# Deltanet and a SiLU feed-forward on one core: the keys of chunk 0 read in long runs, their lengths on GpSimd, and the diagonal blocks taken from PSUM

## The chip, the core and the metric

The kernel runs on one core of a Trainium2 chip. The metric is the device time of one execution in microseconds (us). The core has a matrix engine (TensorE, PE in the profile, its weight loads PEld), a vector engine (VectorE, DVE), a scalar engine (ScalarE, ACT), a general engine (GpSimd, POOL) and a queue engine (SyncE, SP). Each runs its own instructions in order and waits for the others through semaphores. SBUF holds tiles of up to 128 partitions; PSUM receives what TensorE computes.

## What is computed

Four batches of eight heads, 768 tokens, 48 channels a head. For each head a state of 48x48 is carried along the tokens; keys are divided by their lengths:

```python
k_n = k / (np.linalg.norm(k, axis=-1, keepdims=True) + 1e-06)
for t in range(S):
    y[:, :, t] = q_t @ state
    state = state + beta_t * outer(k_t, v_t - state @ k_t)
x = y as 3072 tokens x 384;  h = x @ w_in;  g = h * sigmoid(h);  out = g @ w_out
```

w_in is 384x2048 and w_out 2048x384, both float32.

## The kernel before, in words

**Tiling.** The tokens are cut into 6 chunks of 128 (C, NCH). Inside a chunk the recurrence is solved as a matrix problem: per head a triangular 128x128 system made of k's scores, the lengths and beta is inverted, and then applied to v, to the state and to the queries. The inverse starts from blocks of 32x32 tokens (T) on the diagonal, four to a chunk (NB), and joins them. Chunks 1 to 5 overlap with the feed-forward, whose matmuls (`phid`, L1088, and the output products at L1200) keep TensorE filled to the end of the kernel. Chunk 0 has nothing to overlap with, and the change is in its first part.

**Who sets the order.** The order of instructions on each engine is written out by hand: `pin` (L78) chains an instruction behind the one before it on its engine, `in_line` and `issue` (L92, L101) chain the DMAs on SP's queue (or put one on ACT's). `busy(n)` (L343, L347) issues n matmuls of 128x384 whose results nobody reads. `pin` also counts TensorE's instructions, and the list `loads` (L1504) starts weight and query fetches from the third weight fetch on at given counts, by `paced`.

**Chunk 0's first part (L1445 to L1538).** k comes by six DMAs on SP (`load_pair`, L144) with a token on each partition and a head's 48 floats (192 bytes) as a run, into `kbufs[0]`, whose rows are padded from 48 to 64. beta comes by six DMAs on ACT's queue. Then, in this order of data: POOL squares k (L385); DVE adds up the squares over the channels (`add_squares`, L389) and does sixteen small instructions for lengths and steps (`norm_steps`, L395 to L426, among them the reciprocal at L419, the product at L423 and the transpose of the step at L426); TensorE transposes k with its padding (`turn`, L510) into PSUM, ACT and DVE copy that out (L524, L522); TensorE forms the scores of k with k in 64x64 blocks (`first_score`, `score`, L539); ACT and DVE copy them from PSUM to SBUF (L554, L557); POOL and ACT copy the 32x32 diagonal blocks out of these copies into `stage` (`diagonal_blocks`, L564); DVE turns them so that each partition holds one block of one head (`turn_diagonal`, L578). beta is turned to tokens by a matmul and an ACT copy (`beta_of`, L361, L364).

**The inverse.** `invert_first` (L692) runs on DVE: a multiply by the step (L697), then 15 rank-1 steps of a multiply (L705) and an add each, on both 16x16 halves of every block at once; two transposes (L720 the second); meanwhile TensorE transposes queries and keys of chunk 1 and the dummies of `busy` fill its gaps after steps 9, 11, 13 and 14. Then come the joins on TensorE, each with copies by ACT and DVE behind it: `corner` (L743, the masked adds at L750), `turned` (L759), `straight` (L772), `merge_half` (L832), and then the inner products (L866) and the first outputs (L910). In between ACT, DVE and POOL split the weights into parts ("narrowing": ACT at L233 and L234, POOL at L246), one piece of the weights after another, as they land.

**SP's queue in the first 50 us:** k of chunk 0 (6 DMAs), q (6), the first weight fetch, k of chunk 1 (6), the second weight fetch, v (8), and, at counts of TensorE, the third and fourth weight fetches and the next q.

## Time and profile before

| what | us |
|---|---|
| median of 3 runs | 633.36 (632.27 to 634.15) |
| the profiled execution | 633.96 |
| its span | 631.8 |

The profiled execution is one more run, with the profiler on. Its span goes from the first to the last record; 2.16 us lie around it. The times on the timeline count from the span's start. The mean granted TensorE clock was 0.989 of full speed.

How to read the lines further down: a line of a timeline has start, duration, engine, line of the kernel, operation, output and inputs by the program's names with partitions x elements, and how many instructions it stands for; in brackets the engine's idle time before it and what ended that. Tiles share memory, so one name can stand for several uses: `stage` and `sums_of_w` hold chunk 0's blocks in the first part. One matmul in float32 shows as two records, a transpose as one. A line of the windows has a stretch, its length, the busy time of PE, PEld, DVE, ACT and POOL (number of records), the granted clock (1.00 is full), the busy share of the DMA engines and GB/s; narrowed to one line, it has PE and PEld alone. A line of the chain of waits has start, duration and what the end of the kernel, followed back, hung on. A DMA line of the page has the count, KB each and the median us from issue to landing.

### The profile page before, as it was taken

How to read it: one execution, taken by the hardware profiler on the slowest of the kernel's cores; microseconds unless marked ns; L12 is line 12 of the kernel's file. 1: busy time of each engine (PE TensorE's matmuls, PEld its weight loads, DVE VectorE, ACT ScalarE, POOL GpSimd, SP SyncE). 2: the span in 40 equal slices, each digit the busy share in tenths (PEclk: the TensorE clock that was granted, in tenths of full speed). 3: DMA queues.
4: the chain of work that ended last, by engine and by line, in shares of the span. 5: the costliest groups of instructions: out<-in, count | busy, mean ns of one | idle time of the engine just before them, and what ended most of it. 6: DMA issues, size and time to landing. Idle time of an engine off the chain costs nothing.

```text
span 631.8 us, 21374 instructions
## 1 busy us (share of the span) xinstructions
PE 617.7 (98%) x9390; PEld 543.3 (86%) x9390; DVE 415.5 (66%) x927; ACT 226.7 (36%) x516; POOL 94.0 (15%) x101
## 2 busy tenths in 40 slices
PE   8889989999999999999999999999999999999997
PEld 5578778666799989989989989989989989988997
DVE  6886779999667974546975554976444983345432
ACT  4657873332441122451122451122452122454210
POOL 5234631335020020020020010020002000000000
PEclk9869999999999999999999999999999999999999
DMA  9656506350459360459141359433254024010011
GB/s 175 134 141 199 170 16 149 116 86 4 101 100 186 62 108 4 95 107 188 34 92 20 72 125 156 65 75 44 52 113 95 2 75 62 17 38 1 0 26 26
DMA packets 136941, 52.61 MB, mean 83 GB/s; under 512 B 108672, under 2 KB 130432, under 8 KB 136848
## 3 DMA queue, kind: packets, MB, share of 16 engines
q1 hardware_dynamic: 136512, 51.09, 39.6%
q8 instruction: 74, 1.21, 0.9%
q10 hardware_dynamic: 336, 0.15, 0.1%
q14 instruction: 19, 0.16, 0.1%
HBM read 39.09 MB, written 9.96 MB: 78 GB/s over the span
## 4 chain that ended last, share of the span: by engine, by line
PE 93%; SPq 2%; DMA 1%; issue 1%; ACT 1%; DVE 0%
PE phid L1088 34%; PE px L1200 17%; PE py L1200 13%; PE po L1132 5%; PE pb_c L866 3%; PE pa L539 2%; SPq L144 2%; PE pb_c L1303 2%; PE pb_c L854 2%; PE pyc L945 2%; PE pc L1303 2%; PE pb_c L1132 2%; PE pb_c L886 2%; PE pa L1303 1%; PE pyc L932 1%; PE px L808 1%
## 5 line engine op out<-in xcount | busy, mean ns | idle before, releaser
L1088 PE MATMUL phid<-xT,w_in 128*128 128x256 f32 x960 | 214.9, 382 | 1.9 <-issue 1.7
L1088 PEld LDWEIGHTS phid<-xT,w_in 128*128 128x128 f32 x960 | 180.2, 190 | 26.9 <-issue 2.8
L1098 ACT ACTIVATE gT<-phid 128x512 f32<-128x512 f32 x72 | 42.9, 597 | 115.2 <-PE phid L1088 106.2
L656 DVE SCALAR_TENSOR_TENSOR rank<-g,step,x 128x31 f32<-128x31 f32 (+15 forms) x124 | 49.8, 402 | 23.3 <-DMA g<-blocks 19.8
L1200 PE MATMUL px<-sums_of_w,sums_of_g 128*128 128x192 f32 x320 | 56.6, 329 | 0.0
L1200 PE MATMUL py<-w_out,sums_of_g 128*128 128x192 f32 x320 | 56.2, 328 | 0.0
L1200 PEld LDWEIGHTS px<-sums_of_w,sums_of_g 128*128 128x128 f32 x320 | 52.2, 190 | 0.4
L1200 PEld LDWEIGHTS py<-w_out,sums_of_g 128*128 128x128 f32 x320 | 52.3, 190 | 0.3
L661 DVE TENSOR_TENSOR x<-x,rank 128x31 f32<-128x31 f32 (+15 forms) x124 | 42.5, 342 | 4.3
L477 POOL TENSOR_TENSOR vf<-vf,n_slot 128x768 f32<-128x768 f32 x10 | 14.8, 1492 | 175.4 <-DMA vf<-in_v_dram 129.9
L1183 DVE TENSOR_TENSOR sums_of_g<-gT 128x384 f32<-128x384 f32 (+1 forms) x48 | 24.6, 540 | 14.6 <-ACT gT L1098 14.5
L498 DVE STREAM_TRANSPOSE kq<-stage 128x512 f32<-128x512 f32 x28 | 28.4, 1121 | 6.8 <-DMA stage<-in_q_dram 3.5
L554 ACT COPY xT<-pyc 48x128 f32<-48x128 f32 (+2 forms) x120 | 31.1, 259 | 1.6
L1211 DVE TENSOR_TENSOR o<-o,kept 128x192 f32<-128x192 f32 (+1 forms) x29 | 11.5, 425 | 26.7 <-ACT kept L1208 26.7
L560 POOL COPY g<-x 64x256 f32<-64x256 f32 x4 | 5.0, 1244 | 150.8 <-DVE x L664 150.8
L891 DVE TENSOR_TENSOR state<-state,pb_c 128x384 f32<-128x384 f32 x22 | 11.2, 550 | 24.6 <-PE pb_c L886 24.6
L866 PEld LDWEIGHTS pb_c<-vf,xi 64*64 64x64 f32 x736 | 23.3, 138 | 3.2 <-issue 2.3
L866 PE MATMUL pb_c<-vf,xi 64*64 64x48 f32 x736 | 24.9, 223 | 0.1
L1132 PE MATMUL po<-w_out,gT 128*128 128x384 f32 x64 | 23.7, 491 | 0.0
L1200 PE MATMUL py<-w_out,gT 128*128 128x192 f32 x128 | 23.4, 331 | 0.0
L859 DVE TENSOR_TENSOR vf<-vf,pb_c 128x384 f32<-128x384 f32 x22 | 11.2, 550 | 18.3 <-PE pb_c L854 15.5
L1200 PE MATMUL px<-w_out,gT 128*128 128x192 f32 x128 | 22.4, 327 | 0.0
(293 smaller groups left out, 1094.5 us busy)
## 6 DMA issues: line engine op xcount, KB each, us to landing
vf<-in_v_dram SPq DMA_DIRECT2D x48, 96.0 KB, 2.8
out_dram<-o SPq DMA_DIRECT2D x42, 96.0 KB, 2.2
w_out<-in_moe_w_in_dram SPq DMA_DIRECT2D x4, 768.0 KB, 5.0
sums_of_w<-in_moe_w_out_dram SPq DMA_DIRECT2D x4, 768.0 KB, 4.6
kb<-in_k_dram SPq DMA_DIRECT2D x12, 192.0 KB, 4.5
kb<-in_k_dram SPq DMA_DIRECT2D x24, 96.0 KB, 4.0
raw<-in_moe_w_in_dram SPq DMA_DIRECT2D x3, 768.0 KB, 6.8
blocks<-ap SPq DMA_DIRECT2D x32, 64.0 KB, 1.9
```

What stands on the lines that cost most here:

```text
L477: pin(nc.gpsimd.tensor_tensor(out=vf, in0=vf, in1=of, op=ALU.mult))
L498: pin(nc.vector.transpose(out=kqs[c, b][:, :, j, :].rearrange("p a (i m) -> p a m i", i=T), in_=src.rearrange("p a (m d) -> p a m d", d=D) ...
L554: return pin(nc.scalar.copy(to, of))
L656: pin(nc.vector.scalar_tensor_tensor(out=tv, in0=g[:, 0:m, m : m + 1].to_broadcast([P, m, n]), scalar=step[:, m : m + 1], in1=x[:, m : m + ...
L661: yield pin(nc.vector.tensor_tensor(out=x[:, 0:m, m:T], in0=x[:, 0:m, m:T], in1=tv, op=ALU.add))
L866: yield pin(nc.tensor.matmul(pz[rows, n * D : (n + 1) * D], lhsT=xis[g][rows, u * H + 2 * p + e, :], rhs=vfs[c][rows, hf, g * HB + u, p, : ...
L1088: pin(nc.tensor.matmul(ph[:, j * GT : (j + 1) * GT], lhsT=w_in[:, a, (2 * f + j) * P : (2 * f + j + 1) * P], rhs=xTs[c, hf][:, a, :], star ...
L1098: pin(nc.scalar.activation(out=hidden_of(c, hf, f), in_=ph[:], func=ACTF.Silu, scale=-0.5 if in_blocks(c) else 0.5))
L1132: pin(nc.tensor.matmul(pos[i][:, 0:DM], lhsT=hidden_of(0, hf, f // 2)[:, at : at + C], rhs=w_outs[f // HFF][:, f % HFF, :], start=(f == 0) ...
L1183: pin(nc.vector.tensor_tensor(out=sums_of_g[:, k, fs], in0=of[0], in1=of[1], op=op))
L1200: pin(nc.tensor.matmul(to, lhsT=at, rhs=quarter(f, *b) if isinstance(b, tuple) else sums_of_w[b][:, f], start=start and f == 0, stop=f == ...
L1303: pin(nc.tensor.matmul(to[:, i * GT : (i + 1) * GT], lhsT=left(a, slice(f, f + 1))[:, 0], rhs=right(b), start=start and i == 0 and n == 0, ...
```

## The change

- **k of chunk 0** comes first into `stage`, in runs of 16 tokens (3072 bytes), a partition holding 16 tokens of one head: three DMAs on SP, three on ACT's queue, both at the start. ACT's table load and first activation move behind ACT's three. ACT and DVE copy the runs with padding into `kbufs[0]` (`pad`). beta's six DMAs move to SP behind k, and q follows as a whole. The read of k in the old form (`load_k(0)`, 6 DMAs of 192-byte runs) stays, behind v and ahead of the third weight fetch; its first reader is the update of the state.
- **Squares**: one POOL instruction and one ACT instruction of 128x768; DVE sums each to 128x16.
- **Lengths**: four matmuls (`po`) with a selection matrix `sel`, built by DVE at the start, carry the sums into the layout in which the inverse wants the step (a partition holds a block of a head); ACT copies them out; POOL computes the lengths there in 14 instructions of 128x32, each on the one before; DVE does a reciprocal and a product with beta, which DVE has transposed. The sixteen instructions of `norm_steps(0)` go. POOL's copies of the lengths by token (`n_slot`) come from a transpose behind the inverse's last, and ACT puts the step on the diagonal of x.
- **Transposes and scores**: 16 transposes in four groups, then beta's matmul, the four `po`, then all 64 first scores, where before scores and transposes alternated. `turned_kq` has its axes in another order.
- **Diagonal blocks from PSUM**: per bank one ACT multiply with a 0/1 mask (`halves`) and one DVE multiply-add, four of each; the copies of the scores into SBUF follow, by ACT, 512 columns each. The six ACT and two POOL copies of `diagonal_blocks` go for chunk 0.
- **Dummies**: the first three multiply zeros and need no identity; those after steps 11, 13 and 14 of the inverse (four matmuls) go. Together with the four `po` matmuls that leaves TensorE's count as it was, so the later fetches start at the same instructions.

```diff
--- before.py
+++ after.py
@@ -202,24 +202,42 @@
...
     seen_on = pin(nc.vector.memset(seen[:], 0.0)).ins.engine
+    STEPS = T // 2
+    keys_0 = stage[:, 2 * BH * T + 4 * P :].rearrange("p (e x) -> p e x", e=2)
+    padded_0 = kbufs[0][:].rearrange("p b a e w -> p (b a e w)").rearrange("p (s e w) -> p s e w", e=2, w=W)
+    halves = const.tile([P, 2], FP32, name="halves")
+    for j in range(NB):
+        for i in range(2):
+            pin(nc.vector.memset(halves[T * j : T * (j + 1), i : i + 1], float(j % 2 == i)))
...
+    from_keys = k.rearrange("b (a e) (c i s) d -> e c (b a) i (s d)", e=2, c=NCH, i=2 * NB)
+    for e in range(2):
+        for g in (e, 1 - e):
+            ns = slice(HB * NP * g, HB * NP * (g + 1))
+            m = 2 * NB if g == e else NB
+            for to in range(0, 2 * NB, m):
+                of, at = to if g == e else NB - to, W * g + HB * NP * to
+                issue(
+                    keys_0[at : at + HB * NP * m, e],
+                    from_keys[e, 0, ns, of : of + m].rearrange("n i x -> i n x"), e == 1,
+                )
+    pin(nc.scalar.activation(out=seen[:], in_=seen[:], func=ACTF.Silu))
...
             if e == g:
-                issue(beta_fm[to], of_beta[e][of], True)
+                issue(beta_fm[to], of_beta[e][of])
             else:
                 for hf in range(2):
-                    issue(beta_fm[to, :, 1 - hf], of_beta[e][of, :, hf], True)
+                    issue(beta_fm[to, :, 1 - hf], of_beta[e][of, :, hf])
     load_q(0, slice(0, HB))
+    load_q(0, slice(HB, B))
...
@@ -312,6 +330,12 @@
...
     pin(nc.gpsimd.memset(states[0][:], 0.0))
+    zeros = states[0][:].rearrange("p u a w -> p (u a w)")
+    for _ in range(3):
+        done = pin(nc.tensor.matmul(
+            bank(CC, "pw")[:, 0:DM], lhsT=zeros[:, 0:P], rhs=zeros[:, 0:DM], start=True, stop=True
+        ))
+        tensor.append(done.ins.engine)
...
@@ -333,8 +357,17 @@
...
     second = const.tile([P, 1], FP32, name="second")
-    pin(nc.vector.tensor_reduce(out=second[:], in_=pick[:, T // 2 : T], axis=AX.X, op=ALU.add))
     xi = const.tile([P, 2, HH, W], FP32, name="xi")
+    sel = stage[:, 2 * BH * T : 2 * BH * T + 4 * P].rearrange(
+        "p (e i j g n f) -> p e i j g n f", e=2, i=2, j=NB, g=2, f=2
+    )
+    pin(nc.vector.memset(stage[:, 2 * BH * T : 2 * BH * T + 4 * P], 0.0))
+    for e in range(2):
+        for i in range(2):
+            pin(nc.vector.tensor_copy(
+                out=sel[:, e, i, :, :, :, e],
+                in_=ident[:].rearrange("p (g j i n) -> p i j g n", g=2, j=NB, i=2)[:, i],
+            ))
...
@@ -353,7 +386,6 @@
...
                 after = None
-    pin(nc.scalar.activation(out=seen[:], in_=seen[:], func=ACTF.Silu))
...
@@ -392,6 +424,110 @@
...
     sizes, step_of = {}, {}
+    ss_0 = small.tile([P, 2, STEPS], FP32, name="ss", bufs=1)
+    def half_of(h):
+        return keys_0[:, :, h * STEPS // 2 * D : (h + 1) * STEPS // 2 * D].rearrange("p e (s d) -> p e s d", d=D)
+    def pad(h):
+        for e, by in enumerate((by_act, by_dve)):
+            by(padded_0[:, h * STEPS // 2 : (h + 1) * STEPS // 2, e, 0:D], half_of(h)[:, e])
+    def first_squares(h, by):
+        both = work.tile([P, 2, STEPS // 2, D], FP32, name="sq", tag="gx"[h], bufs=1)
+        of = half_of(h)
+        if by is nc.scalar:
+            pin(by.activation(out=both[:], in_=of, func=ACTF.Square))
+        else:
+            pin(by.tensor_tensor(out=both[:], in0=of, in1=of, op=ALU.mult))
+        return both
+    def first_sums(h, both):
+        pin(nc.vector.tensor_reduce(
+            out=ss_0[:, :, h * STEPS // 2 : (h + 1) * STEPS // 2], in_=both[:], axis=AX.X, op=ALU.add
+        ))
+    def first_turn(h, by):
+        pt = bank(M, "pt")
+        for i in range(4):
+            pin(nc.tensor.transpose(
+                pt[:, C * i : C * (i + 1)], padded_0[:, 4 * h + i].rearrange("p e w -> p (e w)"), ident[:]
+            ))
+        to = turned_kq[:, 0].rearrange("p (g u) a (i s) -> p s g i (u a)", g=2, s=STEPS)[:, 4 * h : 4 * h + 4]
+        of = pt[:].rearrange("p (s g i n) -> p s g i n", s=4, g=2, i=2 * NB)
+        for i, one in enumerate(by):
+            part = slice(4 // len(by) * i, 4 // len(by) * (i + 1))
+            one(to[:, part], of[:, part])
+    def first_step():
+        po = bank(M, "po")
+        for i in range(2):
+            for e in range(2):
+                pin(nc.tensor.matmul(
+                    po[:, STEPS * i : STEPS * (i + 1)], lhsT=sel[:, e, i].rearrange("p j g n f -> p (j g n f)"),
+                    rhs=ss_0[:, e], start=e == 0, stop=e == 1,
+                ))
+        seed, h, r, u = (small.tile([P, BH], kind, name=name, bufs=1)[:] for name, kind in (
+            ("seed", U32), ("nt", FP32), ("nr", FP32), ("nu", FP32)
+        ))
+        ss, n = stage[:, BH * T + T : BH * T + 2 * T], small.tile([P, BH], FP32, name="n", bufs=1)[:]
+        pin(nc.scalar.copy(ss, po[:, 0:T]))
+        pool, root = nc.gpsimd, seed.bitcast(FP32)
+        q = n_2 = root
...
+        plus(seed, ss.bitcast(U32), -0.5, 1597463007.0)
+        plus(h, ss, -0.5, 0.0)
+        product(u, root, root)
+        product(u, u, h)
+        plus(u, u, None, 1.5)
+        product(r, u, root)
+        product(u, r, ss)
+        product(r, u, r)
+        plus(q, r, 0.375, -1.25)
+        product(q, q, r)
+        plus(q, q, None, 1.875)
+        product(u, q, u)
+        plus(n, u, None, 1e-6)
+        product(n_2, n, n)
+        yield
+        step_of[0] = small.tile([P, T], FP32, name="step")
+        pin(nc.vector.reciprocal(out=r, in_=n_2))
+        pin(nc.vector.scalar_tensor_tensor(
+            out=step_of[0][:], in0=r, scalar=-1.0, in1=stage[:, BH * T : BH * T + T], op0=ALU.mult, op1=ALU.mult
+        ))
+        pin(nc.scalar.copy(blocks[0][2].rearrange("p s t -> p (s t)")[:, 0 : T * T : T + 1], step_of[0][:]))
+        yield
+        pin(nc.vector.transpose(out=h, in_=n))
+        of_slots(0, h, nc.gpsimd)
+    def of_slots(c, n, engine):
+        by_slot = small.tile([P, 2, B * NP], FP32, name="n_slot", bufs=1)
+        of = n.rearrange("p (n e) -> p e n", e=2)
+        for g, rows in enumerate(HALVES):
+            ns = slice(HB * NP * g, HB * NP * (g + 1))
+            pin(engine.tensor_copy(out=by_slot[rows, :, ns], in_=of[rows, :, ns]))
+            for hf in range(2):
+                rest = HALVES[1 - g]
+                pin(engine.tensor_copy(out=by_slot[rest, hf, ns], in_=of[rest, 1 - hf, ns]))
+        sizes[c] = by_slot
...
@@ -418,22 +554,21 @@
...
         yield pin(nc.vector.tensor_tensor(out=t, in0=r, in1=beta_tok[:, c, :], op=ALU.mult))
-        if c < 2:
+        if c == 1:
...
             yield pin(nc.vector.transpose(out=step_of[c][:], in_=t))
-            if c == 1:
-                yield
-                yield
+            yield
+            yield
...
             ))
-        engine = nc.vector if c > 0 else nc.gpsimd
+        engine = nc.vector
...
@@ -479,12 +614,12 @@
...
     kqs, aps = {}, {}
-    turned_kq = const.tile([P, B, 2, NP, C], FP32, name="kq")
+    turned_kq = const.tile([P, 2, B, NP, C], FP32, name="kq")
...
         if c != 1:
-            kqs[c, b] = turned_kq[:, b].rearrange("p j a t -> p a j t")
+            kqs[c, b] = turned_kq[:, :, b].rearrange("p j a t -> p a j t")
...
@@ -1057,7 +1192,7 @@
...
     LAST = NCH - 1
-    kq_rows = turned_kq[:].rearrange("p b j a t -> p (b j a t)").rearrange("p (f t) -> p f t", t=2 * GT)
+    kq_rows = turned_kq[:].rearrange("p j b a t -> p (j b a t)").rearrange("p (f t) -> p f t", t=2 * GT)
...
@@ -1442,33 +1577,57 @@
...
-    def first_score(b):
-
-        def evacuate(j, e, to, of):
-            (by_dve if e else by_act)(to, of)
-
-        score(0, b, (0,), (A, CC), evacuate)
-
-    load_q(0, slice(HB, B))
-    busy(3)
+    def first_score(g):
+        aps[0, g] = {
+            j: work.tile([P, HB, H, W], FP32, name=f"ap{j}", tag=f"ap{j}", bufs=2) for j in range(2)
+        }
+        pa = [bank(room, f"pa{e}") for e, room in enumerate((A, CC))]
+        for u in range(HB):
+            kq = kqs[0, g * HB + u]
+            for p in range(NP):
+                for e, hf in ((0, 0), (1, 1), (0, 1), (1, 0)):
+                    rows, half, at = slice(W * e, W * e + D), slice(W * hf, W * (hf + 1)), (u * NP + p) * W
+                    pin(nc.tensor.matmul(
+                        pa[e][half, at : at + W], lhsT=kq[rows, p, 0, half], rhs=kq[rows, p, 0, half],
+                        start=True, stop=True,
+                    ))
+        made = []
+        for e in range(2):
+            of = pa[e][:].rearrange("p (n t) -> p n t", t=W)
+            to = diagonals[0][:, HH * g + e : HH * (g + 1) : 2]
+            pin(nc.scalar.mul(to, of[:, :, 0:T], halves[:, 0:1]))
+            pin(nc.vector.scalar_tensor_tensor(
+                out=to, in0=of[:, :, T:W], scalar=halves[:, 1:2], in1=to, op0=ALU.mult, op1=ALU.add
+            ))
+            made.append((aps[0, g][0][:].rearrange("p u h t -> p (u h) t")[:, e::2], of))
+        return made
     for b in range(B):
-        square(0, b)
+        kq_room(0, b)
+    diagonals[0] = stage[:, 0 : BH * T].rearrange("p (n t) -> p n t", t=T)
+    for h in range(2):
+        pad(h)
+    squares = [first_squares(0, nc.gpsimd), first_squares(1, nc.scalar)]
     block_room(0)
-    add_squares(0, 0)
-    for b in range(2):
-        turn(0, b, 0, M, b % 2 == 0)
-    add_squares(0, 1)
-    first_score(0)
-    for b in range(2, B):
-        turn(0, b, 0, M, b % 2 == 0)
-    add_squares(0, 2)
-    first_score(1)
-    first_score(2)
-    first_score(3)
+    for t in xis:
+        pin(nc.gpsimd.memset(t, 0.0))
+    pin(nc.vector.tensor_reduce(out=second[:], in_=pick[:, T // 2 : T], axis=AX.X, op=ALU.add))
+    first_turn(0, (by_dve,))
+    first_sums(0, squares[0])
+    first_turn(1, (by_act,))
+    first_turn(2, (by_act,))
+    first_sums(1, squares[1])
+    first_turn(3, (by_act, by_dve))
     beta_of(0)
-    diagonal_blocks(0, 0, (by_pool, by_pool, by_act, by_act))
-    diagonal_blocks(0, 1, (by_act, by_act, by_act, by_act))
-    add_squares(0, B - 1)
+    beta_0 = stage[:, BH * T : BH * T + T]
+    pin(nc.vector.transpose(out=beta_0, in_=beta_tok[:, 0, :]))
+    steps = first_step()
+    next(steps)
+    scores = first_score(0) + first_score(1)
+    turn_diagonal(0)
+    for i, (to, of) in enumerate(scores):
+        by_act(to, of)
...
@@ -1481,19 +1640,14 @@
...
     load_v(0)
+    load_k(0)
...
     busy(4)
-    for _ in norm_steps(0):
-        pass
+    next(steps)
...
     step = step_of[0]
-    of_step = blocks[0][2].rearrange("p s t -> p (s t)")[:, 0 : T * T : T + 1]
-    pin(nc.gpsimd.tensor_copy(out=of_step, in_=step[:]))
-    turn_diagonal(0)
-    for t in xis:
-        pin(nc.gpsimd.memset(t, 0.0))
...
@@ -1527,13 +1681,12 @@
...
         done = next(inv)
-        if n in (9, 11, 13):
-            busy(2 if n < 13 else 1, done, Sync)
+        if n == 9:
+            busy(2, done, Sync)
         if n in (6, 8, 10, 12):
             turn(1, n // 2 - 3, 0, M)
-        if n == 14:
-            busy(1, done, Sync)
     corner, turned, straight = next(inv)
+    next(steps, None)
...
```

11 lines of the change are left out of this document (9 added, 2 removed).

## The prediction

> **What bounds the kernel now.** I read the page first: its span, its busy line and its last chain.
>
> ```profile
> span 631.8 us, 21374 instructions
> PE 617.7 (98%) x9390; PEld 543.3 (86%) x9390; DVE 415.5 (66%) x927; ACT 226.7 (36%) x516; POOL 94.0 (15%) x101
> PE 93%; SPq 2%; DMA 1%; issue 1%; ACT 1%; DVE 0%
> ```
>
> PE is busy for 98% of the span and carries 93% of the chain that ended last. The change leaves PE's work after the first 50 us alone, so it can only move the moment at which that work starts. So next: DVE's timeline of the first 32 us (columns: start, duration, engine, line, operation).
>
> ```profile
> 15.45 0.35 DVE L419 RECIPROCAL nr<-n 128x32 f32<-128x32 f32 x1
> 16.18 0.19 DVE L423 SCALAR_TENSOR_TENSOR nt<-nr,nt 128x32 f32<-128x32 f32 x1
> 16.54 1.98 DVE L578 STREAM_TRANSPOSE sums_of_w<-stage 128x1024 f32<-128x1024 f32 x1
> 18.55 0.69 DVE L697 TENSOR_TENSOR sums_of_w<-sums_of_w,step 128x512 f32<-128x512 f32 x1
> 28.92 1.95 DVE L720 STREAM_TRANSPOSE sums_of_w<-sums_of_w 128x1024 f32<-128x1024 f32 x1
> 31.92 0.34 DVE L750 SCALAR_TENSOR_TENSOR sums_of_w<-pl,second,pick 64x128 f32<-64x128 f32 x1 [1.05 <-PE pb_c L743]
> ```
>
> The inverse runs on DVE alone from 18.55 (L697) to 28.92+1.95 = 30.87, and DVE's 1.05 us of idle time before L750 is a wait for PE's corner (L743). PE's timeline shows what the corner waited for:
>
> ```profile
> 29.78 1.46 PE L347 MATMUL pb_c<-state,ident 128*128 128x384 f32 x4
> 31.16 0.20 PE L743 MATMUL pl<-sums_of_w,ap 32*32 32x16 f32 x2
> ```
>
> The last dummies (L347, four passes from 29.78 on) keep the corner until 31.16, 0.29 us after its data. Then the chain of waits, in order of time, shows the other paths into this place:
>
> ```profile
> 25.26 0.89 ACT w_in L233
> 31.38 0.90 ACT raw L234
> 34.80 1.13 issue
> ```
>
> A side path runs through ACT: it narrows the weights that the second fetch brought (from 25.26), and the next ones until 31.38+0.90 = 32.28. From the corner on, PE's order sets the pace, with stalls in which PE waits for nothing shown (34.80). I take it that whatever the corner gains reaches the end, provided the side path gains as much.
>
> **The change, part by part.** *When the keys are there.*
>
> ```profile
> 0.80 4.76 SPq L144 DMA_DIRECT2D kb<-in_k_dram  x6
> kb<-in_k_dram SPq DMA_DIRECT2D x24, 96.0 KB, 4.0
> sums_of_w<-in_moe_w_out_dram SPq DMA_DIRECT2D x4, 768.0 KB, 4.6
> 6.23 1.61 POOL L385 TENSOR_TENSOR sq<-kb 128x384 f32<-128x384 f32 x2 [1.95 <-DMA kb<-in_k_dram]
> 9.00 1.61 POOL L385 TENSOR_TENSOR sq<-kb 128x384 f32<-128x384 f32 x2 [1.15 <-DMA kb<-in_k_dram]
> ```
>
> POOL's squares wait for the two halves of k until 6.23 and 9.00. After, the same 768 KB come in six DMAs of long runs, three on each of two queues. SP took 4.76/6 = 0.79 us an issue, so the third goes out at 0.80+2x0.79 = 2.4 and lands at best with the 4.0 us counted from 1.4 (5.4), at worst at 2.4+4.6 = 7.0; the low end is 0.80+4.0 = 4.8. I take 5.4, since 768 KB of long runs in one DMA needed 4.6. *From keys to scores*, with the durations of the nearest forms:
>
> ```profile
> 12.18 0.54 DVE L389 TENSOR_REDUCE ss<-sq 128x8 f32<-128x384 f32 x1
> 8.34 0.59 ACT L524 COPY kq<-pt 128x512 f32<-128x512 f32 x1 [2.50 <-PE pt L510]
> 6.39 1.91 PE L510 MATMUL pt<-ident,kb 128*128 128x128 f32 x8
> 9.12 1.06 PE L510 MATMUL pt<-ident,kb 128*128 128x128 f32 x8
> 89.99 0.41 PE L1706 MATMUL pg<-pick,ident 128*128 128x32 f32 x2
> 10.11:12.30 2.19, 1.63 (x96) 1.49 (x96) 1.00 1.37 159
> ```
>
> Pads (two 128x384 copies each on ACT and DVE, some 0.5 by the rows of 256 columns below) run to 6.4; POOL's square from 5.4 to 7.0, ACT's to 7.3. PE's 16 transposes (1.06 us per eight, 1.91 when slow) fill four banks that ACT and DVE empty in 0.59 us each, to 9.0. DVE reduces twice 768 columns, each about 2x0.54 less one start, 0.95: one 128x512 copy to 7.4, then 8.35, then 9.3. beta's DMAs, now behind k on SP, land beside this. The four new po matmuls follow: eight passes at 0.41/2 or, overlapped, 0.17: 1.4 us, to 10.7. Then 128 passes of first scores (the last row, first score line alone: 96 took 1.63): 2.2 us, to 12.9. *Blocks from PSUM:*
>
> ```profile
> 17.47 0.37 ACT L554 COPY ap<-pa 128x256 f32<-128x256 f32 x1 [0.31 <-PE pb_c L539]
> 9.13 0.42 DVE L557 COPY ap<-pb_c 128x256 f32<-128x256 f32 x1 [0.43 <-PE pb_c L539]
> 12.30 3.75 ACT L554 COPY stage<-ap 32x512 f32<-32x512 f32 x6
> ```
>
> The six ACT copies of 3.75 us leave the path. Four masked ACT copies and four DVE adds come in; half lie beside the scores. Behind the last score stand two ACT copies (0.37+0.27) and one DVE add (0.42): 14.0. The transpose L578, unchanged, takes 1.98: 16.0; reciprocal and product (0.35+0.19, with gaps 0.55): L697's multiply starts at **16.6**, not 18.55: **-1.95**. Bounds: 16.0 with k at 4.8; 18.2 with k at 7.0.
>
> *Lengths on POOL.* Sixteen norm instructions leave DVE; POOL gets 14 in a chain, each on the one before.
>
> ```profile
> 16.75 0.25 POOL L1493 COPY sums_of_w<-step 128x32 f32<-128x32 f32 x1
> ```
>
> ACT's copy of po ends at 11.0. 14x0.28 (0.25 and a gap of 0.03) = 3.9: 14.9, hidden under the transpose until 16.0. The cover is gone at (16.0-11.0)/14 = 0.36 us an instruction; beyond that each 0.1 costs 1.4. The lower end is DVE's 0.19 (the product at 16.18); no row shows a POOL instruction reading the result just written, so the upper end is twice the 0.25. The Trainium skill, GPSIMD Engine Reference, 4.1 Engine selection, calls GpSimd about 2x slower than VectorE on two-input elementwise work; by that the chain takes about 14x2x0.19 = 5.3, an estimate, and ends at 16.3, so the sum would lose 0.3 and come to 631.5.
>
> *Dummies.* The busy() matmuls after steps 11, 13 and 14 go; the corner then waits for DVE alone: 0.29 less a handover of some 0.05, **-0.23**. Before, three dummies waited for the identity; now they take zeros and start sooner. *Nothing* is charged for: building sel and halves (DVE idles until k lands, 5.4); the lengths' way back to token layout and POOL's n_slot (behind the inverse; v is first scaled when the joins run); ACT's score copies, now behind the muls. Were that cover gone, each costs its own 0.4 to 2 us. On the side path, the 4096 short packets of k that go from the head of the queue free about 2 us of DMA time, so the fetch that landed at 25.26 lands near 23.5, and without the dummies PE's last turn is sooner too. It keeps up.
>
> *Second read of k(0).* Six more DMAs on SP, behind v and ahead of the third weight fetch.
>
> ```profile
> 10.64 7.50 SPq L144 DMA_DIRECT2D kb<-in_k_dram  x6
> 5.61 4.32 SPq L144 DMA_DIRECT2D z<-in_q_dram  x6
> 19.79 6.51 SPq L198 DMA_DIRECT2D vf<-in_v_dram  x8
> 33.12 4.36 SPq L292 DMA_DIRECT2D w_out<-in_moe_w_in_dram  x2
> ```
>
> SP was free from 26.3 to 33.12. Six such issues take 4.3 to 7.5; from about 24.3 they end at 28.6 to 31.8, and the third fetch is due 2.2 before 33.12, at 30.9. I take the short one, since nothing else is then in flight: hidden.
>
> *Clock* (granted clock is the third column from the right; PE busy the second):
>
> ```profile
> 25.49:28.90 3.41, 2.63 (x11) 1.48 (x11) 3.07 (x11) 3.08 (x5) 0.63 (x1) 1.00 0.59 108
> 32.32:35.73 3.41, 2.32 (x151) 1.99 (x139) 2.93 (x7) 1.45 (x4) 1.56 (x2) 1.00 0.39 89
> 39.14:42.56 3.42, 3.07 (x85) 3.00 (x85) 2.22 (x5) 2.25 (x4) 0.06 (x1) 0.50 0.96 280
> 42.56:45.97 3.41, 3.41 (x92) 3.41 (x90) 3.24 (x6) 0.84 (x2) 0.00 (x0) 0.50 0.24 43
> 44.90 1.26 PE py L910 x46
> 47.18 0.94 PE py L910 x46
> ```
>
> In stretches of 3.41 us the clock stayed full after 2.63 busy, was halved after 2.32, stayed halved after 3.07 and was released after 3.41. The same 46 matmuls took 1.26 and 0.94 us: 1.34. Without its dummies the stretch before the corner has about 1.2 busy, so the joins may run halved, up to 2.32x0.34 = +0.8; the dense stretch comes 2 us sooner, so the release may too, 3.41x(1-1/1.34) = -0.9. I take 0, bounds +0.8 and -0.9.
>
> **Sum:** -1.95-0.23 = -2.2. The profiled execution took 633.96 (span 631.8 and 2.16 around it), 0.60 above the median 633.36. So 631.8 against its own time, **631.2** against the median.
>
> **The rivals.** *More than that*: the release one stretch sooner (-0.9): -3.1, 630.3. For: the dense PE stretch after 40. Against: its edges need not stand where they did.
>
> *POOL is the bound*: at 0.50 an instruction the chain ends at 18.0 and the multiply starts at 18.55, so only the 0.23 is left: 633.1. For: dependent instructions. Against: two independent copies on POOL are close to DVE's durations. Here the change moves the wait, and does not remove it.
>
> *The clock stays halved from the first transposes through the scores and the joins.* po 2.7 and scores 2.95 in place of 1.4 and 2.2 (+2.05), joins +0.8: 631.2+2.85 = 634.1. It decides when the early dummies don't fill a stretch. For: they are only three. The Trainium skill, TensorE: Matmul & The Clock Gate, section on what is happening, says that the window is free-running and doesn't start with the kernel; the trace's steps agree in spacing, and where the edge falls no run here shows.
>
> *Slower: the second read of k(0) holds the third weight fetch.* If SP's six issues end at 26.3+7.5 = 33.8, the fetch goes out 2.9 late and, sharing the engines, lands 1.8 later still; ACT is in order, so the copies of xi behind its narrowing wait one for one: -2.2+4.7 = +2.5, 635.9. It decides from about 0.5 us past 30.9. Against: half of the earlier traffic is gone by then.
>
> **How the numbers follow.** Forecast 0.45, more 0.15, POOL 0.15, halved clock 0.12, the held fetch 0.13. The range 629.7 to 634.2 leaves out the held fetch and a little below. A measurement of this kernel can tell about 0.3%, 1.9 us: the forecast lies just past that line, with two thirds of its chance beyond it. Faster 0.15+0.3 and a little of the others, 0.47; slower 0.12; same 0.41. One sign holds most of it.
>
> **What would show it.** POOL's square starting near 5.4; L697's successor near 16.6 right behind reciprocal and product (if it waits for POOL, that rival); DVE's wait before the corner gone; SP's third fetch near 31; the granted clock from 6 to 13 and from 29 to 46. Wrong if the multiply comes sooner and the end does not.

## The result, and the profile after

The changed kernel takes 641.31 us (median of 4 runs, 638.84 to 643.69) against 633.5 of the kernel before in the same runs: ratio 1.0125, 95% interval 1.0082 to 1.0169. It is slower by 7.8 us; the forecast was 2.2 us faster. The profiled execution took 640.42, its span 638.7.

The page of the changed kernel, the same three lines as before:

```profile
span 638.7 us, 21392 instructions
PE 620.1 (97%) x9390; PEld 546.6 (86%) x9390; DVE 415.3 (65%) x928; ACT 228.3 (36%) x520; POOL 94.5 (15%) x109
PE 93%; DVE 3%; DMA 1%; issue 1%; ACT 0%; ACTq 0%; DVEq 0%
```

PE has the same 9390 matmuls and still carries the chain; DVE has come in with 3%, most of it the inverse, in front of which the chain now runs through the DMA of the keys. DVE's timeline of the first 40 us (the pads are the copies into kb; L713 is the old L578, L832 the old L697, L885 the old L750):

```profile
9.94 1.90 DVE L692 COPY kb<-stage 128x384 f32<-128x384 f32 x2 [5.20 <-DMA beta_fm<-in_beta_dram]
11.84 1.01 DVE L692 COPY kq<-pt 128x512 f32<-128x512 f32 x1
22.18 1.98 DVE L713 STREAM_TRANSPOSE sums_of_w<-stage 128x1024 f32<-128x1024 f32 x1
24.63 0.69 DVE L832 TENSOR_TENSOR sums_of_w<-sums_of_w,step 128x512 f32<-128x512 f32 x1
36.92 0.30 DVE L885 SCALAR_TENSOR_TENSOR sums_of_w<-pl,second,pick 64x128 f32<-64x128 f32 x1
39.85 0.42 DVE L692 COPY xe_y<-pb_c 32x256 f32<-32x256 f32 x1 [1.51 <-PE pb_c L894]
```

DVE waits 5.20 us for a DMA and pads the keys at 9.94, where the prediction had 5.4. (The row names beta's DMA, but the pads read only the keys; the same wait of e3, further down, names theirs.) The inverse starts at 24.63, not at 16.6, and 6.1 us later than before. The masked adds (L885) start 5.0 us later than before (31.92). The first copy of the joins starts 6.4 us later than in the kernel before, where it was

```profile
33.49 0.42 DVE L557 COPY xe_y<-pb_c 32x256 f32<-32x256 f32 x1
```

The span has grown by 6.9 us, so nearly all of the loss is there by then. PE's timeline of the changed kernel's first part:

```profile
10.45 1.94 PE L457 MATMUL pt<-ident,kb 128*128 128x128 f32 x8 [4.86 <-DVE kb L692]
13.00 1.94 PE L457 MATMUL pt<-ident,kb 128*128 128x128 f32 x8 [0.61 <-DVE kq L692]
15.20 1.89 PE L471 MATMUL po<-ss,stage 128*128 128x16 f32 x8
```

Both groups of eight transposes take 1.94 us, the slow price of the two quoted in the prediction (1.91 and 1.06). The trace's records of the granted clock begin with a full clock at 23.84 in the changed kernel, and at 8.43 in the kernel before. Ahead of the first record the windows print 1.00, whatever the clock was, so the durations have to be read there. How busy the DMA engines were while everybody waited, in the changed kernel and then in the kernel before (the last two columns are the DMA share and GB/s):

```profile
5.00:6.00 1.00, 0.59 (x1) 0.00 (x0) 0.00 (x0) 0.00 (x0) 0.00 (x0) 1.00 0.31 99
7.00:8.00 1.00, 0.00 (x0) 0.00 (x0) 0.00 (x0) 0.00 (x0) 0.00 (x0) 1.00 0.27 103
```

```profile
5.00:6.00 1.00, 1.00 (x3) 0.34 (x1) 0.00 (x0) 0.83 (x2) 0.00 (x0) 1.00 1.14 172
7.00:8.00 1.00, 1.00 (x7) 0.90 (x5) 0.91 (x2) 0.00 (x0) 0.84 (x2) 1.00 1.21 180
```

With nothing but the keys and beta to fetch, the 16 engines are busy for 0.27 of the time, about four of them, and move 103 GB/s; with the short runs of the kernel before the share was over 1 and they moved 172 to 180. That line became the first theory.

Last, the chain of waits through the joins of the changed kernel:

```profile
37.90 1.28 issue
40.95 1.96 issue
45.34 1.14 issue
```

Before there were two such stalls of PE, 1.13 (shown in the prediction) and one of 1.14 at 38.35; now there are three, 4.4 us together instead of 2.3.

### The profile page after: what moved, and what is told of

Same layout as the page of the kernel before. It is cut to its first block, busy times and chain, and to the rows that moved or that the text cites. A ratio compares the mean times of both kernels' runs of the same rounds, so it can differ in the third digit from the quotient of the medians.

```text
span 638.7 us, 21392 instructions
## 1 busy us (share of the span) xinstructions
PE 620.1 (97%) x9390; PEld 546.6 (86%) x9390; DVE 415.3 (65%) x928; ACT 228.3 (36%) x520; POOL 94.5 (15%) x109
## 4 chain that ended last, share of the span: by engine, by line
PE 93%; DVE 3%; DMA 1%; issue 1%; ACT 0%; ACTq 0%; DVEq 0%
PE phid L1223 33%; PE px L1335 17%; PE py L1335 13%; PE po L1267 5%; PE pb_c L1001 3%; PE pa L674 2%; PE pb_c L1438 2%; PE pb_c L989 2%; PE pyc L1080 2%; PE pc L1438 2%; PE pb_c L1267 2%; PE pb_c L1021 2%; PE pa L1438 1%; PE pyc L1067 1%; DMA stage<-in_k_dram 1%
## 5 line engine op out<-in xcount | busy, mean ns | idle before, releaser
L1026 DVE TENSOR_TENSOR state<-state,pb_c 128x384 f32<-128x384 f32 x22 | 11.2, 549 | 24.1 <-PE pb_c L1021 24.0
L994 DVE TENSOR_TENSOR vf<-vf,pb_c 128x384 f32<-128x384 f32 x22 | 11.2, 550 | 18.3 <-PE pb_c L989 18.2
```

## The experiments

The kernel before ran again beside each group of kernels, with medians between 633.3 and 634.3; every ratio is against the runs beside it.

**Theory A: the keys' DMAs run on few engines.** A DMA of the change has 8 or 4 runs as its slowest dimension. The Trainium skill, DMA: Bandwidth & Descriptors, section "Why a DMA increments its semaphore by 16 and not by 1", says that a DMA uses the largest number of engines up to 16 that divides the slowest dimension of both sides, and the lowest-numbered ones. By that the two DMAs of 192 KB run on engines 0 to 7 and the four of 96 KB on engines 0 to 3, and the share of 0.27 is 4 of 16. The number of engines agrees in e1, in e2 and in the changed kernel (shares of 1.02, 0.54 and 0.27 for 16, 8 and 4); which engines they were, no view here shows. The rival B: long runs into single partitions are slow.

e1_heads_slowest:

```diff
-        for g in (e, 1 - e):
-            ...
-                issue(keys_0[at : at + HB * NP * m, e],
-                    from_keys[e, 0, ns, of : of + m].rearrange("n i x -> i n x"), e == 1)
+        issue(keys_0[:, e], from_keys[e, 0], e == 1)
```

> The changed kernel with one edit: the keys come by one DMA for each parity of the heads, read with the 16 heads as the slowest dimension and the 8 runs next. Runs, bytes, tiles, queues and all later work are as in the changed kernel, but the keys land in other partitions than the chain wants, so that the values computed are not the reference's. Theory A (the six DMAs of the change run on few DMA engines, because their slowest dimension has 8 or 4 entries): here 16 engines take part, the pads start near 5.2 instead of 9.6 us, and the kernel takes some 4 to 6 us less than the changed one, 635 to 637. Theory B (runs of 3072 bytes into single partitions, or being first on two queues, are slow by themselves): pads near 9.6 and 641 as in the changed kernel.

e2_runs_slowest, the same but for the order of two dimensions:

```diff
-        issue(keys_0[:, e], from_keys[e, 0], e == 1)
+        issue(keys_0[:, e], from_keys[e, 0].rearrange("n i x -> i n x"), e == 1)
```

> As e1_heads_slowest, one DMA for each parity, but with the 8 runs as the slowest dimension and the 16 heads next (values computed again not the reference's). Theory A: 8 engines carry 96 KB each where the busiest of the changed kernel carried 144, at about 25 GB/s each: 3.9 us behind a start near 2.0, pads near 6.2, some 3 us less than the changed kernel, 637 to 639. Theory B: no difference between this and e1, both near 641. Theory C (fewer and larger DMAs help, whatever their order): this and e1 alike and both faster than the changed kernel.

e1 took 637.39 (8 runs; ratio 1.0059, 1.0038 to 1.0081), e2 639.43 (6 runs; 1.0083, 1.0063 to 1.0103). In e1 a window with its DMA share and GB/s, then DVE's timeline and ACT's, where the pads show the landing of the two parities (DVE pads the keys of ACT's queue, ACT those of SP's):

```profile
4.00:5.00 1.00, 1.00 (x3) 0.34 (x1) 0.63 (x5) 0.00 (x0) 0.24 (x2) 1.00 1.02 255
```

```profile
5.15 0.63 DVE L684 COPY kb<-stage 128x384 f32<-128x384 f32 x2 [0.41 <-DMA stage<-in_k_dram]
```

```profile
6.75 0.92 ACT L681 COPY kb<-stage 128x384 f32<-128x384 f32 x2 [3.76 <-DMA stage<-in_k_dram]
```

The same three views of e2:

```profile
6.00:7.00 1.00, 0.00 (x0) 0.00 (x0) 0.36 (x2) 0.00 (x0) 0.00 (x0) 1.00 0.54 147
```

```profile
6.64 0.63 DVE L684 COPY kb<-stage 128x384 f32<-128x384 f32 x2 [1.90 <-DMA stage<-in_k_dram]
```

```profile
9.77 0.93 ACT L681 COPY kb<-stage 128x384 f32<-128x384 f32 x2 [6.19 <-DMA stage<-in_k_dram]
```

The same bytes in the same runs: share 1.02 with 16 as the slowest dimension, 0.54 with 8, 0.27 where the changed kernel had 4. Theory A holds, and B and C fall: e1 and e2 differ in the order of two dimensions alone. The sizes were off. In e2 the last keys came at 9.77, not 6.2, and so no sooner than in the changed kernel, since eight engines moved 147 GB/s, 18 each, and not the 25 I had put. Its time lies just above the 637 to 639 expected, with an interval that overlaps the changed kernel's. In e1 the time fell by 3.9 us, just short of the 4 to 6 expected: the keys of SP's queue, with beta behind them, came at 6.75.

**The clock.** e3_warm keeps PE busy until the keys land:

```diff
-    for _ in range(3):
+    for _ in range(7):
         done = pin(nc.tensor.matmul(bank(CC, "pw")[:, 0:DM], lhsT=zeros[:, 0:P], ...
...
-    busy(4)
```

> The changed kernel with seven of the zero matmuls at the start instead of three, and without the four dummies before the first query scores, so that the count of PE's instructions in front of the joins is the same. Theory: the 16 transposes, po and the scores ran at half clock (1.94, 1.94, 1.89 and 3.7 us) because PE was idle from 5.6 to 10.4 us; with PE kept busy to 11 us they take about 1.1, 1.1, 1.4 and 2.2, the inverse starts 2 to 3 us sooner than 24.6, and the kernel takes about 638 to 639. Rival: the clock comes up no sooner, because dummies at half clock do not change the window in which the scores fall, or the copies by ACT and DVE set the pace of the transposes; then the inverse starts within 0.7 us of 24.6 and the time stays near 641.

It took 643.96 (4 runs; ratio 1.0160, 1.0138 to 1.0182), no less than the changed kernel (the intervals overlap), and its inverse started at 26.35, 1.7 us later: the expectation failed, and usefully. PE's timeline of e3, DVE's, and a window (the granted clock is the third column from the right):

```profile
10.46 1.07 PE L457 MATMUL pt<-ident,kb 128*128 128x128 f32 x8 [2.05 <-DVE kb L692]
14.76 1.94 PE L457 MATMUL pt<-ident,kb 128*128 128x128 f32 x8 [3.24 <-DVE kq L692]
```

```profile
9.95 3.68 DVE L692 COPY kb<-stage 128x384 f32<-128x384 f32 x2 [5.21 <-DMA stage<-in_k_dram]
```

```profile
13.25:16.66 3.41, 1.90 (x9) 1.60 (x9) 3.00 (x5) 0.77 (x1) 1.26 (x2) 0.50 1.20 186
```

The first eight transposes ran at full clock, 1.07; then PE stood for 3.24 us behind DVE, the clock was halved (0.93 in the stretch from 9.84 to 13.25, 0.50 in the next), and the second eight took 1.94. What held PE was DVE's pads, 3.68 us for two copies that took 0.63 together in e1. In e3 one took 0.36 and the other 3.40; in the changed kernel 0.36 and 1.62. POOL's timeline of the changed kernel shows what stood beside them:

```profile
10.07 1.55 POOL L444 TENSOR_TENSOR sq<-stage 128x768 f32<-128x768 f32 x1 [5.79 <-DMA beta_fm<-in_beta_dram]
11.57 1.16 POOL L727 MEMSET sums_of_w<- 128x1024 f32 x1
```

The second pad starts beside POOL's square (10.07 to 11.62) and ends at 11.83; in e3 it lasted to 13.62, past the square and into POOL's memsets, which ended at 14.51. The Trainium skill, SBUF — State Buffer, section "Who interferes with whom", has it that VectorE and GpSimd share a port pair, and that beside a VectorE instruction in a two-port mode, as a copy can be, whoever issues first holds the pair for the whole instruction while the other is fully blocked. The 0.36 against 1.62 agrees; 3.40 covers more than one instruction of POOL.

e5_squares_on_act:

```diff
-    squares = [first_squares(0, nc.gpsimd), first_squares(1, nc.scalar)]
+    squares = [first_squares(0, nc.scalar), first_squares(1, nc.scalar)]
```

> The changed kernel with both squares on ACT; POOL's square of 128x768 is gone, so POOL does its memsets before the keys land. Theory: the second of DVE's two pads took 1.63 us (0.36 the first) because it stood beside POOL's square from 10.07 to 11.62 and ended with it; without POOL there it takes 0.36, the first copy out of PSUM starts about 1 us sooner than 11.84, the inverse 0.5 to 1 us sooner than 24.6, and the kernel gains 0.5 to 1. Rival: DVE's pad was slow for another reason (the landing of the last keys); then it stays at 1.6 and the time is the same, or worse by ACT's 0.85.

639.80 (6 runs; ratio 1.0078, 1.0053 to 1.0104), about 1.5 less than the changed kernel's median, with intervals that overlap. With POOL's square gone, both pads together take the time of e1:

```profile
10.47 0.63 DVE L692 COPY kb<-stage 128x384 f32<-128x384 f32 x2 [5.01 <-DMA beta_fm<-in_beta_dram]
```

In this execution the keys landed 0.5 us later than in the changed kernel's, so the inverse started at 24.91, no sooner.

**All three together.** e6_three_cures: e1's edit and e5's, and

```diff
-    for _ in range(3):
+    for _ in range(4):
...
-    busy(4)
+    busy(3)
```

> Keys with the heads slowest as in e1_heads_slowest (values not the reference's), both squares on ACT as in e5, and four zero matmuls at the start instead of three with one dummy less before the first query scores. Theory (three causes: few DMA engines, POOL against DVE, and a clock still halved through transposes, po and scores): the clock is released by 8.5 us, the transposes take 1.06 a bank pair instead of 1.94, po 1.4, the scores 2.2, and the inverse starts at 17.5 to 18.5 (21.3 in e1); the kernel takes 632 to 634, 3 to 5 us less than e1. Rival (the copies out of PSUM by ACT and DVE, 1.0 us each, set the pace whatever the clock): the inverse starts near 20.5 and the time is within 1 us of e1's 637.4.

636.02 (12 runs; ratio 1.0023, 1.0003 to 1.0042). DVE's timeline of e6, and its chain of waits:

```profile
18.09 0.69 DVE L824 TENSOR_TENSOR sums_of_w<-sums_of_w,step 128x512 f32<-128x512 f32 x1
30.38 0.32 DVE L877 SCALAR_TENSOR_TENSOR sums_of_w<-pl,second,pick 64x128 f32<-64x128 f32 x1
33.48 0.92 DVE L684 COPY xe_y<-pb_c 32x256 f32<-32x256 f32 x2 [1.65 <-PE pb_c L886]
```

```profile
31.38 1.42 issue
34.63 1.90 issue
```

Half of it came true. The inverse starts at 18.09, as expected and before the kernel before's 18.55, the masked adds at 30.38, 1.5 sooner than 31.92. Yet the first copy of the joins stands at 33.48, where it stood before (33.49), and the kernel is slower than the one before, if only by a little. The gain is given back inside 3 us, in PE stalls. One cure was not complete: DVE's pads met POOL's memsets and took 2.29 us (two pads from 5.37 on), which cost nothing there, since PE's first transposes waited for ACT's pads of the keys that came at 6.71. So the last question was what paces the joins.

**The dummies, on the kernel before.** e4 and e8 move the four late dummies:

```diff
-        if n in (9, 11, 13):
-            busy(2 if n < 13 else 1, done, Sync)
+        if n == 9:
+            busy(2, done, Sync)
...
-        if n == 14:
-            busy(1, done, Sync)
```

e4_before_less_dummies has busy(7) for busy(3) at the start, e8_before_moved_dummies busy(6) for busy(4) and busy(4) for busy(2) later.

> The kernel before, with the four dummies behind steps 11, 13 and 14 of the inverse moved to the first dummies (seven instead of three), all else as it was. Theory: the corner needs only the first of the two last transposes, and the dummies kept it 1 us longer than my 0.23 us; the first masked add of the corner starts 1.0 us sooner than 31.9 and part of that reaches the end, 632.5 to 633.2. Rival (the joins behind the corner wait for PE's instructions or for ACT's narrowing anyway): the masked adds start sooner, the first copy behind them does not, and the time is within 0.3 of 633.4 or later by what the seven early dummies cost (the transposes of k start near 9 instead of 6.4 us, up to +2).

> The kernel before with the four dummies behind steps 11, 13 and 14 of the inverse moved to the two later groups before it (six instead of four, four instead of two), where PE waits for q. Theory: the corner starts as soon as the first of the two last transposes is done, the masked adds 1.1 us sooner than 31.9, the start of the inverse stays at 18.55, and 0.5 to 1.5 us of it reaches the end: 632 to 633. Rival (the joins are paced by PE's instruction stalls or by ACT's narrowing): masked adds sooner, joins no sooner, 633.9 within 0.4.

e4: 634.96 (12 runs; ratio 1.0031, 1.0009 to 1.0053). Its early dummies put the inverse's start at 21.50, 2.95 late, but the masked adds only 1.8 late (33.69); the median is 1.1 later (the execution with the profile took 638.39, well over it). e8: 633.05 (12 runs; ratio 0.9982, 0.9962 to 1.0003), an interval that just takes in no change. Its inverse starts at 18.50 and its masked adds at

```profile
30.72 0.31 DVE L750 SCALAR_TENSOR_TENSOR sums_of_w<-pl,second,pick 64x128 f32<-64x128 f32 x1
32.41 0.42 DVE L557 COPY xe_y<-pb_c 32x256 f32<-32x256 f32 x1 [0.25 <-PE pb_c L759]
```

1.2 us sooner than 31.92, and here the first copy follows, 1.1 sooner. So dropping the late dummies is worth about 1.1 at the corner, not 0.23, because the corner reads the first of the two last transposes alone. That transpose in the kernel before, and then the corner in e8:

```profile
28.01 1.06 DVE L716 STREAM_TRANSPOSE sums_of_w<-sums_of_w 128x512 f32<-128x512 f32 x1
```

```profile
29.09 0.20 PE L743 MATMUL pl<-sums_of_w,ap 32*32 32x16 f32 x2 [0.63 <-DVE sums_of_w L716]
```

In the kernel before the corner's data was there at 29.07, and the dummies kept it to 31.16: 2.1 us, not 0.29. In e6 something else takes the gain back.

**Theory D: the second read delays PE's code.** e9_no_second_read, e10_three_cures_no_second_read:

```diff
     load_v(0)
-    load_k(0)
```

e11_three_cures_second_read_late puts it into the list of paced fetches behind the next queries:

```diff
+        (WINDOW + PACKET * 5 + 20, load_k, 0),
```

> The changed kernel without the second read of chunk 0's keys (768 KB in 4096 runs of 192 bytes); the update of the state then reads the first, padded form, so its values are not the reference's. Theory D: in the kernel before, the DMA engines stand nearly still from 28 to 34 us, and the code that PE needs for the joins arrives then; with the second read at 30 to 36 us it arrives late (PE's stalls at 37.90 and 40.95, 1.28 and 1.96 us, 3.2 together, where the kernel before has one of 1.13). Without the second read the first stall goes, the first copies of the joins come 1 to 1.5 us sooner behind the corner, and the time falls by 1.5 to 2.5, to 639 to 640. Rival (the stalls come from where the blocks of code begin, or from the corner that starts sooner): both stalls stay, time near 641.

> e6_three_cures without the second read (values not the reference's). Theory D: PE's stall of 1.42 us at 31.38 goes and that of 1.90 at 34.63 shrinks to about 1; the copies of the joins come 1 to 2 us sooner, 634 to 635 less 0 to 1, so 633.5 to 634.5, level with the kernel before or just under it: what is left of the change once its three costs are cured is the 0.5 us by which the inverse starts sooner and the 1.1 us of the dummies. Rival: stalls and time as in e6 (636.0).

> e6_three_cures with the second read moved from behind v to behind the next chunk's queries, near 54 us (values not the reference's, because of the order of the first read). Theory D: the joins run as in e10; the read then stands between other fetches and delays the fifth weight fetch by up to 4 us, of which nothing to 2 us reaches the end: 633.5 to 636. Rival: no different from e6, 636.0.

e9: 642.43 (5 runs; ratio 1.0124, 1.0095 to 1.0153). e10: 635.66 (12 runs; 1.0034, 1.0015 to 1.0053). e11: 639.21 (9 runs; 1.0064, 1.0035 to 1.0094). None is faster than its parent beyond the spread, and e11 is slower. In e9 DVE's pads took 3.67 and the inverse started at 27.02, 2.4 later than in the changed kernel, while the end came 1.1 later; in e10 the first two stalls are 1.22 and 1.54 against e6's 1.42 and 1.90, the third 1.41 against 1.14. In e11 the late read brings two new stalls further on, at 54.66 and 59.10 (0.48 and 1.95). Theory D, as the reason why e6 gains nothing, falls.

**Theory E: PE's code comes in blocks, and its time hangs on the last turns.** Between the ends of two stalls stands the same number of PE's records, here in the kernel before and then in the changed one (windows from the end of one stall to the end of the next; matmuls, then weight loads):

```profile
35.92:39.48 3.56, 2.43 (x127) 2.29 (x128) 3.41 (x7) 2.04 (x5) 1.83 (x1) 0.50 0.62 183
```

```profile
39.17:42.90 3.73, 1.76 (x128) 1.67 (x128) 2.86 (x6) 1.45 (x4) 1.73 (x2) 0.73 0.56 161
42.90:46.47 3.57, 2.43 (x128) 2.29 (x127) 2.70 (x6) 2.11 (x5) 1.84 (x1) 0.50 0.46 118
```

So PE seems to get 256 instructions at a time, run out, and stall until the next 256 come. The DMA view shows something come. The page of the changed kernel has, with the number of packets and MB:

```profile
q8 instruction: 74, 1.21, 0.8%
```

These are 74 packets of 16384 bytes each, and PE's 9390 matmuls and 9390 weight loads are 73.4 times 256. Three of the packets move from 36.54 to 37.73, from 40.25 to 41.48 and from 44.00 to 45.07, and PE's three stalls end at 39.18, 42.91 and 46.48: 1.4 to 1.5 us after each packet. In all kernels the stalls behind the masked adds end 1.3 to 1.7 us after such a packet (2.0 once, in e14). Between two such stalls the next packet starts 1.0 to 1.3 us after the end of the first (0.6 once, in e14). Whose instructions a packet holds, the view does not say, and why no further block is there in advance stays open. But if they are PE's, the joins can't go faster than their code comes, however early the inverse ends, and it matters when the first of those blocks comes. In e6, e9, e10, e11 and the changed kernel it came 4.1 to 5.3 us after PE's last turns (the transposes of chunk 1's keys), which themselves wait for ACT, busy with the first weights: in the changed kernel (ACT's timeline, then PE's)

```profile
32.65 0.96 ACT L251 ACTIVATE w_in<-raw 128x768 f32<-128x768 f32 x1
```

```profile
35.01 1.14 PE L645 MATMUL pt<-ident,kb 128*128 128x128 f32 x8 [0.67 <-ACT stage L659]
```

The last turns at 35.01 and the first stall's end at 39.18. In the kernel before the dummies stood between the turns and the corner while such a packet came (29.05 to 30.33), and covered this. e12_before_turns_first edits e8, e13_three_cures_turns_first edits e6:

```diff
-    begin(("in", 0))
     inv = invert_first(step)
...
             turn(1, n // 2 - 3, 0, M)
+        if n == 12:
+            begin(("in", 0))
```

> e8_before_moved_dummies with one more edit: ACT's narrowing of the first weights starts behind the copies of the last turns of chunk 1's keys, not ahead of them, so that PE's last turns need not wait for it. Theory E (the joins are paced by PE's code, which comes block by block, about 3.57 us apart, and the first block that the joins need comes some 4 us after PE has reached the last turns): last turns near 25.5 instead of 27.3, PE's stalls in the joins end at 34.4 and 38.0 at the latest instead of 35.09 and 38.66, and 0.3 to 0.8 us of that reaches the end, 632.3 to 632.8. Rival (the joins wait for DVE's inverse and the copies, or for the narrowing itself): stalls end where they did, 633.05 or up to 1 us more.

> e6_three_cures with the same edit (values not the reference's, because of the order of the first read). In e6 the inverse started 0.46 us and the joins 1.5 us sooner than in the kernel before, but PE's stalls ended at 32.80, 36.53 and 40.10, no sooner than the kernel before's 35.93 and 39.49. Theory E: the last turns come near 25.5 instead of 27.5, the first stall ends at 31 instead of 32.8 and the next ones 1 to 1.8 us sooner, and the time falls by 1 to 1.8 from 636.0, to 634.2 to 635.0. Rival: the stalls do not hang on the last turns; 636.0 within 0.5.

e12: 632.55 (12 runs; ratio 0.9990, 0.9975 to 1.0005), where its parent e8 had a ratio of 0.9982. e13: 634.29 (12 runs; ratio 1.0021, 1.0005 to 1.0037), where its parent e6 had 1.0023. The medians are 0.5 and 1.7 under the parents', but the kernel before was 0.65 lower beside them, and by the ratios neither is told from its parent. The chain of waits of e13, then of e12:

```profile
29.90 0.82 issue
34.31 1.15 issue
38.05 1.26 issue
```

```profile
29.46 0.79 issue
33.76 0.92 issue
37.12 1.14 issue
```

In e13 the stall of 1.42 in front of the first copies is gone (the one at 29.90 lies beside DVE's transpose), the copy stands at 32.64, and two stalls are left in the joins as in the kernel before; they end at 35.46 and 39.31, 1.1 and 0.8 sooner than in e6. e12's end at 34.68 and 38.26, 0.4 sooner than e8's. The last turns came at 26.81 in e13 and 25.90 in e12, 0.7 and 1.4 sooner than in the parents. So the stalls moved the way that Theory E said, by less than expected, and that any of it reaches the end is not shown. It was tried by moving the turns, not by moving the code, so that blocks of code are what PE waits for is inferred from the counts and the packets. One run more took the second read out of e13, by the edit of e9:

> e13_three_cures_turns_first without the second read of chunk 0's keys (values not the reference's). In e13 PE's stalls ended at 35.46 and 39.31, 3.85 apart, where kernels without other DMA traffic there had 3.57. Theory: the second read, in flight at 26 to 32 us, delays PE's code; without it the stalls end 0.5 to 1 us sooner, at 34.6 to 35.0 and 38.2 to 38.6, and the time falls by 0.4 to 1.0 from 634.3. Rival: the read costs nothing; 634.3 within 0.4, as e10 stood to e6 (635.66 to 636.02).

e14: 633.96 (12 runs; ratio 1.0012, 0.9993 to 1.0031), 0.3 under e13: not to be told from nothing. Its stalls end at 35.73 and 38.91, later than the theory had them. The second read costs nothing that these runs can measure.

e12 has the lowest median of all and e8 the lowest ratio, both with intervals that just take in no change; so none of the kernels is shown to beat the one before. Of those that keep the change, the best (e14) is level with it; it puts the keys into other partitions than the chain wants and leaves out the second read, so it is a measure of time alone.

## Why the prediction was wrong

- **When the keys are there** is the step that failed. I bounded the landing by 4.8 and 7.0 from DMAs of 768 KB and of 96 KB, all of which had a slowest dimension of 16 or more entries and ran on all engines. The six new ones have 8 or 4, and by the shares they ran on eight engines and then on four (0.55 from 4 to 5 us, 0.27 from 6 to 9). The pads started at 9.57 and 9.94: 4.2 over the 5.4, and outside the bounds. e1 and e2 show the cause.
- **From keys to scores** was mis-sized because its cover went. I priced transposes, po and scores mostly at full clock; PE was idle from 5.6 to 10.4 and all of them ran at the slow price. From the keys to po it took 15.20-9.57 = 5.6 instead of 3.9 (two groups of transposes of 1.94, DVE's pad of 1.62, the copies out of PSUM 1.01 instead of 0.59), and po and the scores 5.6 (to the last masked copies by ACT, at 20.76) instead of 3.6. My rival of the halved clock had the mechanism, and 2.05 of the price, but I set it beside the forecast as a case of its own, though late keys bring it on. With PE kept busy ahead of the keys, the first eight transposes took 1.07 in e3 and 1.06 in e6. My reading that a stretch with 3.41 us busy releases the clock is not enough, though: in the changed kernel PE was busy for 3.40 and 3.41 us of the stretches 13.60 to 17.02 and 17.02 to 20.43, and transposes at 20.64 still took 1.97. What releases it stays open.
- With the causes cured the same chain came out nearly as long as forecast: in e6 11.4 us from the keys (6.71) to the multiply (18.09), against 11.2 in the prediction (5.4 to 16.6). Part of that is luck, since po took 1.06 instead of 1.4 and both squares ran on ACT. The sum 16.6 missed by 8.0: 4.2 of landing, 1.7 up to po, 2.0 in po and the scores, and 0.2 behind them.
- **Blocks from PSUM** and **lengths on POOL** held. POOL's 14 instructions ran from 17.40 to 21.88, 0.32 each (0.28 predicted, 0.36 the edge), and ended 2.2 us before the reciprocal that reads them (24.06). The slow scores had widened the cover; in e6, at full clock, they still ended 0.7 before it (16.85 and 17.52). The rival that POOL is the bound did not come.
- **Dummies**: -0.23 was -1.1 (24.63 to 36.92 is 12.3, where it was 13.4), since the corner's data was there at 29.07 and not at 30.87, and the other side of the edit was missed: they also stood where PE would wait for the next code. In the changed kernel the stall at 37.90 gives back 1.3.
- **"Whatever the corner gains reaches the end"** failed in e6: 1.5 us at the corner were gone at the first copy of the joins. I had quoted the stall of 1.13 and taken it for a delay that moves along.
- **The second read** was hidden, as forecast: SP was through with it at 33.84 and the third fetch waited for PE until 39.55. The slower rival named the wrong mechanism for the right sign.
- **The clock** later on: the halved stretch from 40.91 is 13.65 us long, before it was 10.24. I took 0 with bounds of +0.8 and -0.9; it was not measured by itself. In e8, which drops the same dummies from the kernel before and is not slower, it is 13.65 too.

## What to carry to other kernels

A DMA is priced by its shape as well as by its bytes: look in the windows whether the DMA share says that all engines work, and compare with a row of the same slowest dimension, not of the same size. Dummies and waits that look idle may be the cover of something that the timeline does not show (here instruction packets, which the DMA view has); where "issue" stalls end at nearly fixed distances, look for such packets, because an earlier start then moves nothing until what feeds them is earlier too. A term whose price depends on another (the clock on when data lands) belongs in one case with it.

## What the runs showed of the hardware that I had not expected

- The slowest dimension sets how many DMA engines take part: shares of 1.02, 0.54 and 0.27 for 16, 8 and 4 entries, 255 to 350, 147 and 103 GB/s.
- A DVE copy from SBUF to SBUF of 128x384 takes 0.36 us alone; beside POOL's instructions it took 1.62 in the changed kernel and 3.40 in e3 and e9, whose code is the same up to there but for PE's dummies. That this spreads the changed kernel's times (over 4.9 us) is not shown: e5, without POOL's square, spreads over 4.1.
- Where about 256 of PE's records (255 to 258) lie between the ends of two stalls in the joins, these are 3.3 to 4.0 us apart, most often 3.56 to 3.58; one pair does not fit this count (229 records in 3.18 us, in e14).
- PE's stalls in the joins end 1.3 to 1.7 us after a packet of 16384 bytes on the instruction queue (2.0 once).
- Busy time alone did not release the clock: it stayed halved in the changed kernel to 23.84, through two stretches of 3.41 us in which PE was busy for 3.40 and 3.41.
